# Gated mix of linear attention and a GLU on one core: the down products leave PSUM through ScalarE and are summed in DRAM by accumulating transfers, where VectorE summed them in SBUF

## Chip, cores and metric

The kernel runs on one core of a Trainium2 chip. The metric is the device time of one execution in microseconds (us). Lower is better.

## What is computed

Two branches read the same input x (2048 tokens of 640 numbers, float32) and a gate per token mixes them:

```python
g = sigmoid((x * gate_w).sum(-1, keepdims=True))
a = linear_attention(x, wqkv, wo)        # 32 heads of 20, phi(t) = where(t > 0, t + 1, exp(t)) + 1e-6
b = (sigmoid(x @ w_gate) * (x @ w_up)) @ w_down     # 640 -> 1536 -> 640
return g * a + (1 - g) * b
```

The change concerns b, above all its last product ("down"), and the way b comes to the final mix.

## The kernel before

**Layout.** Everything is kept transposed: features on the 128 partitions, tokens along the free axis. 640 features are KC = 5 chunks of 128, 1536 hidden features are FC = 12 blocks of 128, and 2048 tokens are NG = 4 groups of TG = 512. Groups are worked in pairs, the pair pr = 1 (groups 2 and 3) first and then pr = 0 (groups 0 and 1). A float32 operand is split into a high part (ScalarE copy to fp32r) and a low part (VectorE subtraction), and each product is three matmuls: high by high, high by low, low by high (`mm3`, L183 to L187).

**Stages.** First the keys. Then for each pair a q phase (`q_phase`, L1252), which makes phi(q) and stores it in DRAM (`p_dram`; in the q phase of pr = 1 the small matrix M, the heads' key-value products times wo, is made as well and written to `m_dram`), and an f phase (`f_phase`, L1271). The f phase walks through the 12 hidden blocks f. For each it takes seven steps s1 to s7 that make the gate and up products of both groups, with partial sums of the operands formed beforehand by VectorE. Steps s1, s3 and s5 each leave something in the PSUM tile "ch" that ScalarE copies out before TensorE goes on in the same tile: the copy of s1 has to be done before s3 starts, with s2 between them.

**The down product.** After s5 of each f from 2 on, five down units are worked (L1309 to L1312): one token group, all five output chunks o. A unit is `down_unit` (L1240): six matmuls with the weights of two hidden blocks, into a PSUM tile "rot" or "dd" (two buffers each). Its result is added to b of that group and chunk: the first pair of hidden blocks (f = 0) is copied by ScalarE into the SBUF tile `tb`, every later one is added to `tb` by VectorE (L1246 to L1250). So there are 20 batches of five units, ten in each f phase. The last two hidden blocks are done by `last_down` (L1331): ten units in a row, the first halves of the first four of them ahead. That makes 120 units in all. In the pair pr = 1, `last_down` also sends each finished chunk of `tb` to `b_dram` (L1342, issued by GpSimd), since `tb` is used again by the pair pr = 0.

**Between the pairs.** `last_down` of pr = 1 runs just ahead of the q phase of pr = 0. Around it ScalarE makes the high parts that this phase needs: `wgh` (the q weights), `xbh`, `b12h` (parts of x); VectorE then the low parts, and from x in the staging tile `xst` the operand sums. When the last of them has been split (`xth`, `xtl`), SP loads the other half of x into the same staging tile (L314).

**The final mix.** For the groups 2, 3, 0, 1 in this order: 25 products M times phi(q) for each group; `scale_b` (L1485) multiplies b by 1 - g (`omg`, read back from `om_dram`); `finish` (L1488) adds the PSUM tile to it, and SP stores it. Groups 2 and 3 read b from `b_dram` (`load_b`, L1447), groups 0 and 1 have it in `tb`. The loads for the third and fourth group are issued after the products of the second and third (L1534 to L1538).

**What sets the order.** The program is written in the order in which each engine runs it. A planner (`Order`, L46) keeps estimated clocks of TensorE, ScalarE and VectorE and drops waiting operand preparations (splits, sums) between the fixed steps where its estimates say that they fit. Each helper (`act`, `vec2` and so on) adds its cost to these clocks, so an operation that changes engine can move others. Each engine runs its list strictly in order. Transfers are issued by SP, except those from tiles that GpSimd issues (`p_dram`, `m_dram`, `om_dram`, `b_dram`). Tiles with `bufs=n` rotate: a writer waits until the last user of the buffer is done.

Of the kernel before, what the change touches and what calls it, by code (L numbers as in the profile page):

```python
# [7 lines left out]
F32 = mybir.dt.float32  # L8
F32R = mybir.dt.float32r
I32 = mybir.dt.int32  # L10
AF = mybir.ActivationFunctionType
OP = mybir.AluOpType
# [3 lines left out]
P = 128  # L16
S, D, F = 2048, 640, 1536
H, DH = 32, 20
KC = D // P
FC = F // P  # L20
TG = 512
NG = S // TG
# [134 lines left out]
def v_cost(w):  # L157
    return 0.155 + w * 0.00104
# [3 lines left out]
def gated_mix_kernel(ctx: ExitStack, tc: tile.TileContext, xt, xn, wk, wv, wo, wst_q, wst_f, out_t):  # L162
    nc = tc.nc
# [4 lines left out]
    dram = ctx.enter_context(tc.tile_pool(name="scratch", bufs=1, space=DRAM))  # L168
# [5 lines left out]
    def width(ap):  # L174
        n = 1
        for s in ap.shape[1:]:
            n *= s
        return n

    def ps_tile(tag):  # L180
        return psum.tile([P, 512], F32, name=tag, tag=tag, bufs=2)
# [7 lines left out]
    def prod(out, terms, first):  # L189
        for n, t in enumerate(terms):  # L190
            mm3(out, *t, first and n == 0, n == len(terms) - 1)


    def act(out, src, fn, after="", **kw):
        order.on_act(width(out), after)
        nc.scalar.activation(out, src, fn, **kw)  # L196

    def vec2(out, a, b, op, after=""):
        order.on_vec(width(out), after)
        nc.vector.tensor_tensor(out, a, b, op=op)  # L200
# [21 lines left out]
    def add(out, a, b, after=""):  # L222
        vec2(out, a, b, OP.add, after)
# [12 lines left out]
    logit_l = common.tile([P, S // P], F32R, name="logit_l")  # L236
    fac = common.tile([P, NG, TG], F32, name="fac")
    p_dram = dram.tile([P, KC, NG, TG], F32, name="p_dram")
    b_dram = dram.tile([P, KC, 2, TG], F32, name="b_dram")
    om_dram = dram.tile([P, NG, TG], F32, name="om_dram")  # L240
    m_dram = [dram.tile([D, D], F32, name=n) for n in ("mh_dram", "ml_dram")]
    bdn = HPG * DH
# [468 lines left out]
    g = GTBatch(0, [0])  # L711
# [8 lines left out]
    for c in range(1, 4):  # L720
# [66 lines left out]
        g = GTBatch(c, batches[c])  # L787
# [44 lines left out]
    def tt(name, dt=F32, shape=(P, TG)):  # L832
        return pw.tile(list(shape), dt, name=name, tag="t", bufs=4)

    def ct(name, dt=F32, shape=(P, TG)):
        return pw.tile(list(shape), dt, name=name, tag="c", bufs=5)
# [320 lines left out]
    down_pool = []  # L1157
    HT, DST, WD = {}, {}, {}
    d_loads = [n for n in entries if n[0] == "f"]
    tb = None  # L1160

    def load_d():
        if d_loads:
            n = d_loads.pop(0)
            t = down_pool[0].tile([P, D], F32, name="dst", tag="dst", bufs=2)
            nc.sync.dma_start(t, wst_f[n[2], :, 2])
            DST[n] = (t, order.pe + 4.0)
# [10 lines left out]
    def queue_d(n):  # L1178
        if not down_pool:
            waiting_d.append(n)  # L1180
            return
        order.add(a_cost(D), v_cost(D), lambda: split_d(n), ("d", n), lambda: DST[n][1])
# [9 lines left out]
    other = []  # L1192

    def m_close():
        nonlocal tb
        mp_cm.__exit__(None, None, None)
        m1_cm.__exit__(None, None, None)
        kp_cm.__exit__(None, None, None)
        down_pool.append(ctx.enter_context(tc.tile_pool(name="down", bufs=1, reuse_waits="tile")))
        tb = down_pool[0].tile([P, KC, 2, TG], F32, name="tb")  # L1200
        load_d()
        load_d()
        for n in waiting_d:
            queue_d(n)
        xst2 = down_pool[0].tile([P, 2, KC, CW], F32, name="xst2", tag="xst2")
        other.extend(Next(0, i, xf, i * CW, xst2, True) for i in range(2))
        other[0].load()
# [27 lines left out]
    def down_term(ps, pr, f, o, g, first):  # L1235
        os_ = slice(o * P, (o + 1) * P)
        h, l = WD["f", pr, f]
        mm3(ps, h[:, os_], l[:, os_], *HT[f, g], first, not first)

    def down_unit(pr, f, o, g, ps=None):  # L1240

        if ps is None:
            ps = ps_tile("rot" if (o + g) % 2 else "dd")
            down_term(ps, pr, f, o, g, True)
        down_term(ps, pr, f + 1, o, g, False)
        dst = tb[:, o, g]  # L1246
        if f == 0:
            act(dst, ps, AF.Copy, "p")
        else:
            add(dst, ps, dst, "p")  # L1250

    def q_phase(pr, b12, extra):  # L1252

# [77 lines left out]
    def last_down(pr, units):  # L1331
        order.need(("d", ("f", pr, FC - 1)))
        early = []
        for i in units[:4]:
            g, o = divmod(i, KC)
            early.append(ps_tile("rot" if (o + g) % 2 else "dd"))
            down_term(early[-1], pr, FC - 2, o, g, True)
        for i in units:
            g, o = divmod(i, KC)
            down_unit(pr, FC - 2, o, g, early.pop(0) if early else None)  # L1340
            if pr:
                nc.gpsimd.dma_start(b_dram[:, o, g], tb[:, o, g])  # L1342
            order.fill()

    order.need((nx[1], 2))
# [60 lines left out]
    groups = (2, 3, 0, 1)  # L1406
    PL, PQ, BL, OMG, MHL = {}, {}, {}, {}, {}

    def x2_tile(name, dt=F32):
        return px.tile([P, 2, TG], dt, name=name, tag="x2", bufs=10)  # L1410

    def x3_tile(name, dt=F32):
        return px.tile([P, 3, TG], dt, name=name, tag="x3", bufs=4)
# [18 lines left out]
    def load_p(g):  # L1432

        if groups.index(g) % 2 == 0:
            t = down_pool[0].tile([P, KC, TG], F32, name="pl", tag="xst2")
            nc.sync.dma_start(t, p_dram[:, :, g])
            PL[g] = [t[:, u] for u in range(KC)]
        else:
            PL[g] = []
            for u in range(0, KC, 2):  # L1440
                t = x2_tile("pl")
                w = min(2, KC - u)
                nc.sync.dma_start(t[:, :w], p_dram[:, u:u + w, g])
                PL[g] += [t[:, i] for i in range(w)]
        PL[g, "at"] = order.pe + 6.0

    def load_b(g):  # L1447

        OMG[g] = tt("omg")
        nc.sync.dma_start(OMG[g], om_dram[:, g])  # L1450
        if g < 2:
            BL[g] = [tb[:, o, g] for o in range(KC)]
        elif g == groups[0]:
            BL[g] = [ct("bl") for _ in range(KC)]
            for o in reversed(range(KC)):
                nc.sync.dma_start(BL[g][o], b_dram[:, o, g - 2])
        else:
            t = [x3_tile("bl") for _ in range(2)]
            nc.sync.dma_start(t[0], b_dram[:, 0:3, g - 2])
            nc.sync.dma_start(t[1][:, 0:2], b_dram[:, 3:5, g - 2])  # L1460
            BL[g] = [t[o // 3][:, o % 3] for o in range(KC)]

    def pq_scale(g, u):
        p = PL[g][u]
# [2 lines left out]
    def pq_tiles(g):  # L1467

        if groups.index(g) % 2 == 0:
            t = [x2_tile("pq", F32R) for _ in range(5)]  # L1470
            PQ[g] = [(t[u // 2][:, u % 2], t[2 + u // 2][:, u % 2]) for u in range(4)] + [(t[4][:, 0], t[4][:, 1])]
        else:
            t2 = [x2_tile("pq", F32R) for _ in range(2)]
            t3 = [x3_tile("pq", F32R) for _ in range(2)]
            PQ[g] = [tuple(t[:, u] for t in t2) for u in range(2)] + [tuple(t[:, u] for t in t3) for u in range(3)]

    def queue_scale(g, lazy=False):
        for u in range(KC):
            order.add(0, v_cost(TG), lambda u=u: pq_scale(g, u), ("sc", g), lambda: PL[g, "at"], lazy=lazy)

    def queue_pq(g):
        for u in range(KC):
            order.add(a_cost(TG), v_cost(TG), lambda u=u: split(*PQ[g][u], PL[g][u]), ("pq", g, u))

    def scale_b(g, o):  # L1485
        vec2(BL[g][o], BL[g][o], OMG[g], OP.mult)
# [24 lines left out]
    last_down(0, range(2 * KC))  # L1511
    load_p(groups[2])
    load_b(groups[1])
    for gi, g in enumerate(groups):
        for u in range(KC):
            order.need(("pq", g, u))
        for o in reversed(range(KC)):
            order.add(0, v_cost(TG), lambda o=o: scale_b(g, o), ("b", g, o), first=True)
        if 0 < gi < NG - 1:
            nxt = groups[gi + 1]  # L1520
            queue_scale(nxt)
            pq_tiles(nxt)
            queue_pq(nxt)
        for o in range(KC):
            os_ = slice(o * P, (o + 1) * P)
            cuts = (0, TG // 2, TG) if gi == NG - 1 and o == KC - 1 else (0, TG)
            for c0, c1 in zip(cuts, cuts[1:]):
                ps = ps_tile(("rot", "dd", "cc", "ch")[(o + gi) % 4])
                prod(ps[:, c0:c1], [(MHL[k, 0][:, os_], MHL[k, 1][:, os_], PQ[g][k][0][:, c0:c1],
                                     PQ[g][k][1][:, c0:c1]) for k in range(KC)], True)  # L1530
                order.need(("b", g, o))
                finish(g, o, ps, c0, c1)
            order.fill()
        if gi == 1:  # L1534
            load_p(groups[3])
            load_b(groups[2])
        if gi == 2:
            load_b(groups[3])  # L1538
    for cm in (pw_cm, pg_cm, px_cm):
        cm.__exit__(None, None, None)  # L1540

# [39 lines left out]
```

## Time and profile before

| What | us |
|---|---|
| median of 3 runs (764.15 to 766.01) | 765.08 |
| the profiled execution, its own time | 766.16 |
| span of the profiled execution (first to last instruction) | 764.4 |
| VectorE busy | 559.7 |
| ScalarE busy | 327.1 |
| GpSimd busy | 26.9 |

The profile is that of one execution. The span is 1.8 us shorter than that execution's own time, and that execution is 1.1 us above the median of the runs. "Busy" counts an engine's instructions; a matmul's row ends when its pipeline has drained, so consecutive matmul rows overlap, and the distance from start to start is what one costs. In the rows of a timeline the columns are the start, the duration, the engine, the line of the program, the operation with output <- inputs, the count, and in brackets how long the engine had been idle before it and what ended that.

### The profile page before, as it was taken

Reading aid. Unit: us, or ns where it says so; the run is one execution under the profiler, and the core shown is the slowest. Engines: PE = TensorE matmul, PEld = TensorE weight load, DVE = VectorE, ACT = ScalarE, POOL = GpSimd, SP = SyncE. Lnnn points to the kernel's source line nnn. Section 1 sums busy time; section 2 is a strip of 40 time slices with the busy share of each in tenths; the row PEclk is TensorE's granted clock in tenths of the full one; section 3 lists DMA queues with packets and bytes.
Section 4 is the critical chain, followed back from the end, with each engine's and each line's share of the span. In section 5 each row is a group of like instructions: output and inputs, shape, how many; then the busy total and the mean of one; then the engine's idle time right before and its main releaser. Section 6 shows DMA issues by size and latency. Waiting matters only on the chain.

```text
span 764.4 us, 9852 instructions
## 1 busy us (share of the span) xinstructions
PE 757.3 (99%) x3727; PEld 649.2 (85%) x3727; DVE 559.7 (73%) x988; ACT 327.1 (43%) x603; POOL 26.9 (4%) x55
## 2 busy tenths in 40 slices
PE   9999999999999999999999999999999999999998
PEld 7999999988888888888888878888888888888886
DVE  4888778877776677678878766666776788777664
ACT  4763646356554524333434445555333334231110
POOL 0000000023000000000001210000000000000000
PEclk9999999999999999999999999999999999999999
DMA  7130414597722212121322354322121222455233
GB/s 259 50 123 2 138 37 137 167 273 249 238 97 76 97 49 69 35 84 34 117 69 104 135 186 141 108 76 96 36 69 34 84 104 73 120 178 193 83 128 121
DMA packets 44725, 85.40 MB, mean 112 GB/s; under 512 B 8055, under 2 KB 20855, under 8 KB 44677
## 3 DMA queue, kind: packets, MB, share of 16 engines
q1 hardware_dynamic: 41061, 72.57, 29.4%
q0 software_dynamic: 3616, 12.19, 4.5%
q8 instruction: 29, 0.48, 0.2%
q14 instruction: 19, 0.16, 0.1%
HBM read 67.32 MB, written 17.43 MB: 111 GB/s over the span
## 4 chain that ended last, share of the span: by engine, by line
PE 98%; DMA 1%; ACT 0%; DVE 0%; SPq 0%; issue 0%
PE dd L186 9%; PE dd L185 9%; PE dd L184 9%; PE ch L184 9%; PE ch L185 9%; PE ch L186 9%; PE rot L184 8%; PE rot L185 8%; PE rot L186 8%; PE cc L184 6%; PE cc L186 6%; PE cc L185 6%; DMA wv_sb<-wv 1%; PE ch L1124 1%; DMA xnh<-wk 0%; PE rot L1024 0%
## 5 line engine op out<-in xcount | busy, mean ns | idle before, releaser
L196 ACT ACTIVATE c<-ch 128x512 f32<-128x512 f32 x72 | 43.0, 598 | 151.6 <-PE ch L186 151.4
L200 DVE TENSOR_TENSOR hl<-c,hh 128x512 fp32r<-128x512 f32 x48 | 33.0, 688 | 27.7 <-ACT hh L196 27.7
L196 ACT ACTIVATE c<-c 128x512 f32<-128x512 f32 x48 | 30.1, 628 | 44.6 <-DVE c L200 44.6
L186 PE MATMUL rot<-hh,wdl 128*128 128x512 f32 x120 | 46.8, 390 | 0.0
L186 PE MATMUL dd<-hh,wdl 128*128 128x512 f32 x120 | 46.8, 390 | 0.0
L184 PE MATMUL dd<-hh,wdh 128*128 128x512 f32 x120 | 46.7, 389 | 0.0
L184 PE MATMUL rot<-hh,wdh 128*128 128x512 f32 x120 | 46.7, 389 | 0.0
L185 PE MATMUL dd<-hl,wdh 128*128 128x512 f32 x120 | 46.7, 389 | 0.0
L185 PE MATMUL rot<-hl,wdh 128*128 128x512 f32 x120 | 46.7, 389 | 0.0
L200 DVE TENSOR_TENSOR c<-cc,c 128x512 f32<-128x512 f32 x48 | 32.9, 685 | 18.8 <-ACT c L196 13.8
L200 DVE TENSOR_TENSOR tb<-rot,tb 128x512 f32<-128x512 f32 x52 | 35.8, 688 | 8.9 <-PE rot L186 8.3
L184 PE MATMUL dd<-xrh,wgh 128*128 128x512 f32 x102 | 40.0, 393 | 1.8 <-ACT wgh L196 1.8
L200 DVE TENSOR_TENSOR wsl<-wsum,wsh 128x512 fp32r<-128x512 f32 (+1 forms) x48 | 36.0, 753 | 7.2 <-ACT wsh L196 7.1
L200 DVE TENSOR_TENSOR tb<-dd,tb 128x512 f32<-128x512 f32 x52 | 35.7, 686 | 6.8 <-PE dd L186 6.3
L186 PE MATMUL dd<-xrh,wgl 128*128 128x512 f32 x102 | 39.9, 391 | 0.1
L185 PE MATMUL dd<-xrl,wgh 128*128 128x512 f32 x102 | 39.8, 390 | 0.0
L196 ACT ACTIVATE wsh<-wsum 128x512 fp32r<-128x512 f32 (+1 forms) x48 | 31.8, 678 | 17.4 <-DVE wsum L200 17.4
L200 DVE TENSOR_TENSOR wgl<-wst,wgh 128x640 fp32r<-128x640 f32 x32 | 26.3, 822 | 15.3 <-ACT wgh L196 15.3
L186 PE MATMUL ch<-xth,wsl 128*128 128x512 f32 x96 | 37.5, 390 | 0.0
L184 PE MATMUL ch<-xth,wsh 128*128 128x512 f32 x96 | 37.3, 389 | 0.0
L185 PE MATMUL ch<-xtl,wsh 128*128 128x512 f32 x96 | 37.3, 389 | 0.0
L196 ACT ACTIVATE xth<-xst 128x512 fp32r<-128x512 f32 x24 | 14.3, 626 | 47.5 <-DVE xst L200 47.5
(393 smaller groups left out, 2211.4 us busy)
## 6 DMA issues: line engine op xcount, KB each, us to landing
wst<-wst_f SPq DMA_DIRECT2D x24, 640.0 KB, 3.9
xst<-xt SPq DMA_DIRECT2D x12, 640.0 KB, 6.0
dst<-wst_f SPq DMA_DIRECT2D x24, 320.0 KB, 2.9
xnst<-xn SPq DMA_DIRECT2D x16, 320.0 KB, 3.0
p_dram<-qr POOLq DMA_DIRECT2D x20, 256.0 KB, 3.9
pden<-p_dram SPq DMA_DIRECT2D x20, 256.0 KB, 4.1
b_dram<-tb POOLq DMA_DIRECT2D x10, 256.0 KB, 2.6
pl<-p_dram SPq DMA_DIRECT2D x2, 1280.0 KB, 7.4
```

What stands on the lines that cost most here:

```text
L184: nc.tensor.matmul(out, l_hi, r_hi, start=first, stop=False, skip_group_check=True)
L185: nc.tensor.matmul(out, l_hi, r_lo, start=False, stop=False, skip_group_check=True)
L186: nc.tensor.matmul(out, l_lo, r_hi, start=False, stop=last, skip_group_check=True)
L196: nc.scalar.activation(out, src, fn, **kw)
L200: nc.vector.tensor_tensor(out, a, b, op=op)
L1124: nc.tensor.matmul(ps[:w, :w], v[:, m, :w], gt[:, m, c0:c0 + w], start=(m == 0), stop=(m == KC - 1))
```

## The change

Every down unit is now copied out of PSUM by ScalarE into a small tile `y` (four buffers), and GpSimd issues a transfer of `y` to `b_dram`: for the first pair of hidden blocks it overwrites, for all later ones it adds to what is in DRAM. VectorE's additions and the tile `tb` are gone, `b_dram` has room for all four groups, and the final mix reads b of all groups from `b_dram`. The loads of b and phi(q) for the third and fourth group are issued before the products of the second and third group instead of after them.

```diff
-    b_dram = dram.tile([P, KC, 2, TG], F32, name="b_dram")
+    b_dram = dram.tile([P, KC, NG, TG], F32, name="b_dram")
...
-        tb = down_pool[0].tile([P, KC, 2, TG], F32, name="tb")
...
         down_term(ps, pr, f + 1, o, g, False)
-        dst = tb[:, o, g]
-        if f == 0:
-            act(dst, ps, AF.Copy, "p")
-        else:
-            add(dst, ps, dst, "p")
+        y = y_tile("y")
+        act(y, ps, AF.Copy, "p")
+        nc.gpsimd.dma_start(b_dram[:, o, 2 * pr + g], y, accum_op=OP.add if f else OP.bypass)
+
+    def y_tile(name):
+        return down_pool[0].tile([P, TG], F32, name=name, tag="y", bufs=4)
...
             down_unit(pr, FC - 2, o, g, early.pop(0) if early else None)
-            if pr:
-                nc.gpsimd.dma_start(b_dram[:, o, g], tb[:, o, g])
...
-        if g < 2:
-            BL[g] = [tb[:, o, g] for o in range(KC)]
-        elif g == groups[0]:
-            BL[g] = [ct("bl") for _ in range(KC)]
+        n = groups.index(g)
+        if n == 1:
+            t = [x3_tile("bl") for _ in range(2)]
+            nc.sync.dma_start(t[0], b_dram[:, 0:3, g])
+            nc.sync.dma_start(t[1][:, 0:2], b_dram[:, 3:5, g])
+            BL[g] = [t[o // 3][:, o % 3] for o in range(KC)]
+        else:
+            def tile_of(tag):
+                return down_pool[0].tile([P, TG], F32, name="bl", tag=tag, bufs=4)
+
+            if n == 0:
+                BL[g] = [ct("bl") for _ in range(KC)]
+            elif n == 2:
+                BL[g] = [tile_of("hh") for _ in range(4)] + [tile_of("hl")]
+            else:
+                BL[g] = [tile_of("hl") for _ in range(3)] + [y_tile("bl") for _ in range(2)]
             for o in reversed(range(KC)):
-                nc.sync.dma_start(BL[g][o], b_dram[:, o, g - 2])
...
+                nc.sync.dma_start(BL[g][o], b_dram[:, o, g])
...
+        if gi == 1:
+            load_p(groups[3])
+            load_b(groups[2])
+        if gi == 2:
+            load_b(groups[3])
         for o in reversed(range(KC)):
             order.add(0, v_cost(TG), lambda o=o: scale_b(g, o), ("b", g, o), first=True)
...
-        if gi == 1:
-            load_p(groups[3])
-            load_b(groups[2])
-        if gi == 2:
-            load_b(groups[3])
```

More of the change, by code (lines that the diff above doesn't have):

```diff
@@ L1159, in gated_mix_kernel @@
     d_loads = [n for n in entries if n[0] == "f"]
-    tb = None
     def load_d():
@@ L1194, in m_close @@
     def m_close():
-        nonlocal tb
         mp_cm.__exit__(None, None, None)
@@ L1450, in load_b @@
         nc.sync.dma_start(OMG[g], om_dram[:, g])
-        if g < 2:
-            BL[g] = [tb[:, o, g] for o in range(KC)]
-        elif g == groups[0]:
-            BL[g] = [ct("bl") for _ in range(KC)]
-            for o in reversed(range(KC)):
-                nc.sync.dma_start(BL[g][o], b_dram[:, o, g - 2])
[L1457 to L1461, printed above, removed]
+        n = groups.index(g)
[13 more added lines that the diff above has]
+                BL[g] = [tile_of("hl") for _ in range(3)] + [y_tile("bl") for _ in range(2)]
+            for o in reversed(range(KC)):
+                nc.sync.dma_start(BL[g][o], b_dram[:, o, g])
     def pq_scale(g, u):
```

## The prediction

> **What bounds the kernel now.** I read the page's busy times first, then the chain that ended last, then TensorE's waits.
>
> ```profile
> span 764.4 us, 9852 instructions
> ...
> PE 757.3 (99%) x3727; PEld 649.2 (85%) x3727; DVE 559.7 (73%) x988; ACT 327.1 (43%) x603; POOL 26.9 (4%) x55
> ```
> ```profile
> PE 98%; DMA 1%; ACT 0%; DVE 0%; SPq 0%; issue 0%
> ```
> ```profile
> PE dd L184 <- ACT wgh L196: 1.8, 1, 1.8
> ```
> TensorE is busy 757.3 of 764.4 us and is 98% of the chain. Of its 7.1 idle us the longest single wait in mid-run is one of 1.8 us, for ScalarE's `wgh`. As built, the changed kernel gives TensorE the same matmuls in the same order. So VectorE's saving cannot shorten anything by itself: the change can win at most this 1.8 us, and can lose wherever TensorE meets a later ScalarE or a later transfer. (0.2% of 765.08, 1.53 us, is about what a measurement of this kernel can tell from no change.)
>
> **What is removed and added on the engines.**
>
> ```profile
> L200 DVE TENSOR_TENSOR tb<-rot,tb 128x512 f32<-128x512 f32 x52 | 35.8, 688 | 8.9 <-PE rot L186 8.3
> L196 ACT ACTIVATE tb<-rot 128x512 f32<-128x512 f32 x10 | 6.0, 599 | 3.4 <-PE rot L186 3.0
> ```
> Half of the units come from a rot tile and half from a dd tile; these are the rot rows, and the dd ones are like them. Of the 60 + 60 units, 10 + 10 are copied by ScalarE already and 50 + 50 are VectorE additions (the other 2 in the row belong to the final mix). VectorE loses 100 x 0.688 = 68.8 us, ScalarE gains 100 x 0.599 = 59.9 us and goes from 43% to 51%. Neither is the bound. What counts is whether ScalarE is late, and the trace already has two batches of units (f = 2 and 3 of each pair, which end the pair of hidden blocks f = 0) with ScalarE copies in just the order of the new program:
>
> ```profile
> 246.88 0.60 ACT L196 ACTIVATE tb<-rot 128x512 f32<-128x512 f32 x1 [0.24 <-PE rot L186]
> ...
> 252.33 0.60 ACT L196 ACTIVATE tb<-rot 128x512 f32<-128x512 f32 x1
> 252.82 0.73 ACT L196 ACTIVATE wdh<-dst 128x640 fp32r<-128x640 f32 x1
> 253.69 0.60 ACT L196 ACTIVATE c<-ch 128x512 f32<-128x512 f32 x1
> ```
> ```profile
> 255.54 0.39 PE L184 MATMUL ch<-xth,wuh 128*128 128x512 f32 x1
> ```
> The fifth copy starts 5.45 us after the first (252.33 - 246.88). The copy of "ch" that TensorE needs ends at 254.29, 1.25 us ahead of s3 at 255.54. So the ScalarE work by itself costs nothing in the 20 batches; TensorE's own work hides it.
>
> **The new wait.** `y` has four buffers, so the fifth copy of a batch waits until the first transfer has landed, and on ScalarE the split of `wdh` and the copy of "ch" are queued behind it. ScalarE can slip by the 0.14 us that it idles ahead of "ch" (253.69 less 252.82 + 0.73) and the 1.25 above: 1.4 us. From the end of a copy to its buffer's release there are thus 5.45 - 0.60 = 4.85 us before ScalarE waits, and 4.85 + 1.4 = 6.2 us before TensorE does. Now the transfer:
>
> ```profile
> 417.68 0.69 DVE L200 TENSOR_TENSOR tb<-dd,tb 128x512 f32<-128x512 f32 x1 [0.67 <-PE dd L186]
> ```
> ```profile
> 418.67 0.54 POOL L1342 DMA_DIRECT2D b_dram<-tb  x1 [0.82 <-DVE tb L200]
> ```
> ```profile
> 598.54 0.54 POOL L1054 DMA_DIRECT2D om_dram<-om  x1 [134.47 <-ACT om L196]
> ```
> ```profile
> DMA  0000000000000009997988981000000703000000
> ...
> q0 software_dynamic: 80, 0.26, 23.1%
> ...
> om_dram<-om POOLq DMA_DIRECT2D x1, 256.0 KB, 2.5
> ```
> The first two rows: GpSimd starts 0.30 us after the operation that it waits for (418.67 - 418.37). The other two fences are a plain write of the same 256 KB that is alone, and the 3.0 us from 598.5 on: the transfer engines are busy from slice 15 on (0.075 us each, so 1.08 us after the issue), the write holds all 16 of them for T = 23.1% of 3.0 = 0.7 us, and it lands after 2.5, some 0.7 after its data. A release thus takes 0.30 + 1.08 + T + 0.7 = 2.1 + T: 2.8 us for a plain write.
>
> **What an accumulating transfer holds the engines for is not in this trace.** From below, T = 0.7: the write alone, if the read of b went beside it. From above:
>
> ```profile
> pden<-p_dram SPq DMA_DIRECT2D x20, 256.0 KB, 4.1
> ```
> a read of 256 KB lands after 4.1 us; a read and a write one behind the other, with nothing overlapped, make T = 4.1 + 2.5 = 6.6. It has to fetch 256 KB from DRAM besides moving the 256 KB of `y`, by the same 16 engines; two passes at the row's 0.7 are 1.4. I take T = 1.5, near the row of the plain write, since many packets are in flight at a time. The Trainium skill ("Collectives: The Full Stack", section "The bandwidth ceiling: the fold count and why AG ≠ RS ≠ AR") holds that an add in the transfer path is free, but needs two source reads on one ring, which halves the rate; that would be T = 1.4 as an estimate, and by it the sum below would be 1.3 us in place of 1.9, where the write's row alone gives none; no run here shows it yet. With T = 1.5 the release takes 3.6 us, inside the 4.85: the 20 batches cost nothing.
>
> **The place where it does cost: `last_down` ahead of the q phase of pr = 0.** There ten units come in a row, the second halves of the first four in quick succession, and six transfers queue up before the tenth copy can start.
>
> ```profile
> 413.85 0.39 PE L186 MATMUL dd<-hh,wdl 128*128 128x512 f32 x1
> ```
> ```profile
> 424.05 0.40 PE L186 MATMUL rot<-hh,wdl 128*128 128x512 f32 x1
> ```
> These are the last matmuls of units 1 and 10; a copy starts 0.03 us after such a row ends, as the fifth copy of the batch above does at 252.33:
>
> ```profile
> 251.90 0.40 PE L186 MATMUL rot<-hh,wdl 128*128 128x512 f32 x1
> ```
> The first copy runs from 414.27 to 414.87, and its data starts at 414.87 + 0.30 + 1.08 = 416.25. With transfers behind each other at T each, the sixth lands at 416.25 + 6T + 0.7, and the tenth copy, due at 424.48, needs that buffer: it is late by D = 6T - 7.53 us, if that is positive. For T = 1.5 that is 1.47. A load shares the engines at that time:
>
> ```profile
> q1 hardware_dynamic: 144, 0.33, 7.2%
> ```
> (stretch 414 to 427): the q weights hold the engines for 0.94 us. It may fall wholly behind the sixth transfer or wholly ahead of it; I take half, 0.47. So D = 1.9 us. What is queued behind the tenth copy on ScalarE is the second `b12h`, and from it a chain without slack:
>
> ```profile
> 425.69 0.69 DVE L200 TENSOR_TENSOR b12l<-xs,b12h 128x512 fp32r<-128x512 f32 x1
> 426.29 2.14 DVE L200 TENSOR_TENSOR xst<-xst 128x512 f32<-128x512 f32 x3
> ...
> 435.24 0.69 DVE L200 TENSOR_TENSOR xtl<-xst,xth 128x512 fp32r<-128x512 f32 x1 [0.70 <-ACT xth L196]
> ```
> ```profile
> 435.96 1.24 SPq L314 DMA_DIRECT2D xst<-xt  x2
> ```
> ```profile
> 453.80 0.50 PE L184 MATMUL dd<-xrh,wgh 128*128 128x512 f32 x1 [1.77 <-ACT wgh L196]
> ```
> The sums of x follow `b12l`, the last `xtl` frees the staging tile, SP loads it, the sums from it and their splits precede `wgh` on ScalarE, and there TensorE waits its 1.8 us. With D = 0 the new order reaches the second `b12l` at about 425.6 and the last `xtl` at about 435.2, as before (one more `xth` stands ahead of the table load, one less behind). So this wait becomes 1.8 + D. The other `last_down` has nothing of this kind behind its tenth copy: the copies delay `pq` splits of the second group, whose products come a whole group later.
>
> **Moved loads.** b of two more groups (10 x 256 KB) comes from DRAM, issued ahead of the products of the second and third group.
>
> ```profile
> 726.58 0.69 DVE L200 TENSOR_TENSOR bl<-dd,bl 128x512 f32<-128x512 f32 x1 [2.75 <-PE dd L186]
> 734.53 3.10 DVE L200 TENSOR_TENSOR tb<-tb,omg 128x512 f32<-128x512 f32 x5 [7.26 <-DMA omg<-om_dram]
> ...
> 761.15 0.42 DVE L200 TENSOR_TENSOR tb<-ch,tb 128x256 f32<-128x256 f32 x1 [1.36 <-PE ch L186]
> ```
> ```profile
> bl<-b_dram SPq DMA_DIRECT2D x1, 768.0 KB, 9.5
> ```
> VectorE waited 7.26 us for `omg` here and TensorE did not notice; the loads now start one group of products earlier, and loads like them landed after 9.5 (last fence), ahead of their use. Stores queue behind them on SP, and nobody waits for a store. The last addition waits for TensorE, and no load stands behind it. Zero, then; if this cover were gone, the cost is bounded by the 7 us. GpSimd issues 110 transfers more, 110 x 0.54 = 59 us of an idle engine; the `p_dram` and `om_dram` writes stand behind some of them on GpSimd and would be late only if the queue does not keep up (rival 3).
>
> **Sum.** 764.4 + 1.9 = 766.3 us of span, 766.16 + 1.9 = 768.1 for that execution, which lay 1.1 above the median; on the median 765.08 + 1.9 = **767.0 us**.
>
> **Rivals.**
> 1. *Nothing happens*: T below 1.25, so D = 0: 765.1 us. For it: a plain write takes 0.7. Against it: twice the data to read.
> 2. *Faster*: VectorE, without its ten additions between 414 and 425, forms the operand sums earlier, SP's load at 435.96 moves up, and the 1.8 us wait goes: 763.3 us. It decides from a load 1.8 us earlier on. Against it: the sums stand behind `b12h`, which now stands behind the tenth copy.
> 3. *The queue does not keep up*: a block lasts 245.25 - 226.19 = 19.06 us (rows below) and brings five transfers, so from T = 3.8 on the transfers set the pace of the 20 blocks. At T = 5: 20 x (25 - 19.06) = 119, and D = 22: about 906 us. For it: the upper bound of 6.6.
>
> ```profile
> 226.19 0.23 PE ch L186
> ...
> 245.25 0.23 PE ch L186
> ```
> **How the numbers follow.** Forecast (T from 1.25 to 3.8) 0.56, rival 1 0.24, rival 2 0.08, rival 3 0.12. Of the forecast, 0.10 lies below T = 1.43, within 0.2% even with half of the load's share. Faster 0.08, same 0.24 + 0.10 = 0.34, slower 0.46 + 0.12 = 0.58. Range: from 764.4, half a clearing of the wait, to T = 3.8 (D = 15.7): 781. It leaves out rival 3 and most of rival 2, at most 0.20. The forecast's own range is 765.1 to 781.
>
> **What would show it.** TensorE free of waits in the batches; the fifth copy of a batch at its old place; transfers of `y` landing after about 3.3 us alone; copies nine and ten before the q phase late and the wait for `wgh` at 1.8 + D. It is wrong if landings stay near 2.5 (rival 1), if the x load moves up (rival 2), or if ScalarE waits for transfers in every batch (rival 3).

## The result, and the profile after

| | before | after |
|---|---|---|
| median, us (4 runs each) | 764.82 | 773.32 |
| lowest to highest, us | 764.15 to 766.01 | 772.66 to 776.44 |
| profiled execution: own time, span | 766.16, 764.4 | 773.57, 771.8 |

The changed kernel is slower: ratio 1.0117, 95% interval 1.0087 to 1.0148, about 8.5 us. Direction and range of the forecast held (767.0, range 764.4 to 781), but it expected 1.9 us.

The page of the changed kernel: span, busy time, one DMA queue (packets, MB, share of the 16 engines' span), one group of instructions, and one kind of transfer (count, size, median us to landing).

```profile
span 771.8 us, 10181 instructions
...
PE 759.5 (98%) x3727; PEld 649.1 (84%) x3727; DVE 499.8 (65%) x888; ACT 385.5 (50%) x703; POOL 118.8 (15%) x165
...
q0 software_dynamic: 18816, 41.04, 27.2%
...
L1245 POOL DMA_DIRECT2D b_dram<-y x120 | 97.4, 833 | 370.3 <-ACT y L196 368.8
...
b_dram<-y POOLq DMA_DIRECT2D x120, 256.0 KB, 6.8
```

VectorE lost 59.9 us and ScalarE gained 58.4 (68.8 and 59.9 were worked out from single rows, which overlap where they follow each other closely); by themselves neither shows in the time (experiment 1). What is new is the transfer: GpSimd's queue holds the engines for 27.2% of the span, and a transfer of `y` lands 6.8 us after its issue. TensorE's waits in the changed kernel (total us, times, longest):

```profile
PE dd L184 <- ACT wgh L196: 3.4, 2, 2.2
PE rot L271 <- POOL warm L268: 1.4, 1, 1.4
PE dd L184 <- ACT y L196: 1.3, 1, 1.3
PE rot L184 <- ACT y L196: 1.2, 2, 0.9
PE rot L185 <- DVE b12l L200: 0.3, 1, 0.3
PE rot L184 <- ACT b12h L196: 0.3, 1, 0.3
PE cc L1100 <- DVE ms L200: 0.3, 1, 0.3
```

The second line is the start, the same as before; the last one lies at 191 us, ahead of all transfers of `y`. The others come from two places, the two `last_down` stages. **Where the 7.4 us of span went** can be read off because TensorE runs the same matmuls in the same order in both kernels: take the same matmul in both timelines and subtract. The difference is its lag. First before, then after:

```profile
410.68 0.39 PE L184 MATMUL dd<-hh,wdh 128*128 128x512 f32 x1
...
438.06 0.40 PE L184 MATMUL dd<-xrh,wgh 128*128 128x512 f32 x1
...
440.13 0.39 PE L184 MATMUL dd<-xah,wgh 128*128 128x512 f32 x1
...
691.92 0.39 PE L184 MATMUL rot<-pq,m 128*128 128x512 f32 x1
...
760.83 0.28 PE L186 MATMUL ch<-pq,m 128*128 128x256 f32 x1
```

```profile
409.31 0.39 PE L184 MATMUL dd<-hh,wdh 128*128 128x512 f32 x1
...
429.18 0.38 PE L184 MATMUL rot<-b12h,wgh 128*128 128x256 f32 x1 [0.30 <-ACT b12h L196]
...
440.25 0.62 PE L184 MATMUL dd<-xrh,wgh 128*128 128x512 f32 x1 [2.24 <-ACT wgh L196]
440.67 0.63 PE L185 MATMUL dd<-xrl,wgh 128*128 128x512 f32 x1
...
444.10 0.40 PE L184 MATMUL dd<-xah,wgh 128*128 128x512 f32 x1
...
457.16 0.50 PE L184 MATMUL dd<-xrh,wgh 128*128 128x512 f32 x1 [1.12 <-ACT wgh L196]
...
694.02 0.50 PE L184 MATMUL dd<-hh,wdh 128*128 128x512 f32 x1 [1.32 <-ACT y L196]
...
698.52 0.50 PE L184 MATMUL rot<-pq,m 128*128 128x512 f32 x1 [0.91 <-ACT y L196]
...
767.57 0.28 PE L186 MATMUL ch<-pq,m 128*128 128x256 f32 x1
```

| same matmul, before / after | lag of after | added |
|---|---|---|
| 410.68 / 409.31 | -1.37 | (start) |
| 438.06 / 440.25 | +2.19 | 3.56: waits for `b12h`, `b12l`, `wgh` |
| 440.13 / 444.10 | +3.97 | 1.78: the same matmuls, run slower |
| 453.80 / 457.16 | +3.36 | -0.61: this wait is 1.12 instead of 1.77 |
| 691.92 / 698.52 | +6.60 | 3.24: `last_down` of pr = 0 |
| 760.83 / 767.57 | +6.74 | 0.14: the whole final mix |
| span 764.4 / 771.8 | +7.4 | 0.66: the last stores |

The 1.37 us at the start arise among the first matmuls, which the change does not touch; the profiled execution of before was 1.3 us above its median. Without them the change costs 3.56 + 1.78 - 0.61 = 4.73 us around the q phase, 3.24 us in the last `last_down`, 0.80 us behind it: 8.8 us, against 8.5 between the medians. Nothing is lost in the 20 batches: from 230 to 410 and from 460 to 690 us the lag is constant.

ScalarE in the two places (timeline of the changed kernel):

```profile
412.96 0.60 ACT L196 ACTIVATE y<-dd 128x512 f32<-128x512 f32 x1 [0.70 <-PE dd L186]
...
417.82 0.60 ACT L196 ACTIVATE y<-dd 128x512 f32<-128x512 f32 x1 [2.22 <-DMA b_dram<-y]
...
424.32 0.60 ACT L196 ACTIVATE y<-dd 128x512 f32<-128x512 f32 x1 [0.17 <-DMA b_dram<-y]
...
428.01 0.60 ACT L196 ACTIVATE y<-rot 128x512 f32<-128x512 f32 x1 [2.57 <-DMA b_dram<-y]
428.50 0.62 ACT L196 ACTIVATE b12h<-xs 128x512 fp32r<-128x512 f32 x1
...
687.35 0.60 ACT L196 ACTIVATE y<-rot 128x512 f32<-128x512 f32 x1
693.37 0.60 ACT L196 ACTIVATE y<-dd 128x512 f32<-128x512 f32 x1 [5.42 <-DMA b_dram<-y]
```
```profile
439.36 1.24 SPq L314 DMA_DIRECT2D xst<-xt  x2
```

The fifth copy of each stage waits for the first transfer, and so on. In the prediction's rows the tenth copy was due 424.48 - 414.27 = 10.21 us after the first, so here at 423.17; it starts at 428.01, **D = 4.84 us** late. SP's load of x stands at 439.36 instead of 435.96: 3.40 later, 4.77 with the 1.37 at the start. So the chain handed D on one for one.

A view by stretches (stretch and its length; busy time and count of TensorE, its weight loads, VectorE, ScalarE, GpSimd; TensorE's granted clock; DMA share; GB/s) of the changed kernel shows the slower matmuls as a granted clock of 0.95 between 425 and 460 us:

```profile
425.00:460.00 35.00, 30.86 (x147) 24.99 (x146) 19.63 (x30) 18.01 (x33) 5.56 (x9) 0.95 0.52 147
```

### The profile page after: what moved, and what is told of

Read it like the earlier page. It is cut to its first block, busy times and chain, and to the rows that moved or that the text cites. A ratio compares the mean times of both kernels' runs of the same rounds, so it can differ in the third digit from the quotient of the medians.

```text
span 771.8 us, 10181 instructions
## 1 busy us (share of the span) xinstructions
PE 759.5 (98%) x3727; PEld 649.1 (84%) x3727; DVE 499.8 (65%) x888; ACT 385.5 (50%) x703; POOL 118.8 (15%) x165
## 3 DMA queue, kind: packets, MB, share of 16 engines
q0 software_dynamic: 18816, 41.04, 27.2%
## 4 chain that ended last, share of the span: by engine, by line
issue 42%; PE 35%; POOL 12%; DMA 5%; DVE 4%; ACT 2%; POOLq 0%; SPq 0%; ACTq 0%; DVEq 0%
POOL b_dram L1245 11%; PE rot L184 3%; PE rot L185 3%; PE rot L186 3%; PE ch L185 3%; PE ch L184 3%; PE ch L186 3%; PE dd L186 3%; PE dd L185 3%; PE dd L184 2%; PE cc L184 2%; PE cc L186 2%; PE cc L185 2%; DMA b_dram<-y 2%; DMA xst<-xt 2%
## 5 line engine op out<-in xcount | busy, mean ns | idle before, releaser
L1245 POOL DMA_DIRECT2D b_dram<-y x120 | 97.4, 833 | 370.3 <-ACT y L196 368.8
L196 ACT ACTIVATE y<-dd 128x512 f32<-128x512 f32 x60 | 35.9, 599 | 31.5 <-PE dd L186 20.3
L196 ACT ACTIVATE y<-rot 128x512 f32<-128x512 f32 x60 | 36.0, 599 | 25.9 <-PE rot L186 18.1
L973 POOL DMA_DIRECT2D p_dram<-qr x20 | 11.2, 559 | 212.6 <-DVE qr L204 203.1
```

Source lines behind the costliest of these rows:

```text
L973: nc.gpsimd.dma_start(p_dram[:, u, g], r)
L1245: nc.gpsimd.dma_start(b_dram[:, o, 2 * pr + g], y, accum_op=OP.add if f else OP.bypass)
```

## The experiments

Theory A: the transfers hold the four buffers of `y` too long, and only in the two `last_down` stages does that reach TensorE. Rival B: the transfers hold the 16 engines so long that other loads are late, however many buffers there are. Rival C: the copies make ScalarE late by themselves.

**1. Eight buffers.**

```diff
-        return down_pool[0].tile([P, TG], F32, name=name, tag="y", bufs=4)
+        return down_pool[0].tile([P, TG], F32, name=name, tag="y", bufs=8)
```

> Eight buffers for y instead of four, all else as in the changed kernel. Theory A (the loss is ScalarE waiting for a buffer of y in the two last_down stages: a transfer holds its buffer too long for four of them; 4.8 us ahead of the q phase of pr = 0, 3.2 us in the last_down of pr = 0): the copies 5 to 10 wait for transfers that landed long ago, no wait of ScalarE for a transfer of y is left, TensorE's waits for y and b12h go, the matmuls of 0.63 us at the q phase go, and the time comes back to that of before, 764 to 766 us. Rival B (the transfers hold the 16 DMA engines so long that the loads of x and of the final mix come late, however many buffers there are): at least half of the loss stays, 769 us or more. Rival C (the copies themselves make ScalarE late): no change, 773 us.

Measured: 766.0 us (12 runs), ratio to before 1.002 (1.0005 to 1.0034). The waits of TensorE:

```profile
PE ch L1124 <- DMA wv_sb<-wv: 1.7, 1, 1.7
PE dd L184 <- ACT wgh L196: 1.4, 1, 1.4
...
```

No wait for `y`, `b12h` or a second `wgh` is left. B and C are out as the main cause of the loss: the same copies and the same transfers cost 1.1 us (2.6 at the upper end of the interval) once the buffers suffice. These 1.1 us over before stay open; the wait for `wv_sb` lies at 162 us, ahead of all transfers of `y`, and of the other kernels' profiles some have it (1.4 to 1.5 us) and some do not.

**2. No adding.** `accum_op=OP.bypass` for all transfers; the kernel then leaves out the sum of the parts of b.

> All transfers of y write b plainly instead of adding to it (this leaves out the sum of the parts of b). Theory A: a plain write holds the engines for about 0.7 us instead of about 1.75, so four buffers are enough: 764 to 766 us, no TensorE wait for y. Rival B: the same, 764 to 766, since the transfers then hold the engines for 120 x 0.7 us only. Rival C (copies on ScalarE as such): no change, 773 us.

Measured: 765.16 us, ratio 1.0007 (0.9996 to 1.0018), as A has it; one wait of 0.3 us for `y` is left. Its page, with the same queue line of before behind it, gives the price of the adding (before had 10 transfers of b where there are 120 now, and 100 of these add):

```profile
span 763.5 us, 10181 instructions
...
q0 software_dynamic: 12416, 41.04, 14.1%
...
b_dram<-y POOLq DMA_DIRECT2D x120, 256.0 KB, 2.7
```
```profile
q0 software_dynamic: 3616, 12.19, 4.5%
```

Plain: (14.1% of 763.5 - 4.5% of 764.4) / 110 = 0.67 us of all engines per transfer. Adding: (27.2% of 771.8 - 14.1% of 763.5) / 100 = 1.02 us on top, so T, the time for which one adding transfer holds the engines, is 1.69 us; and 6400 packets more, 64 each.

**3 and 4. One place at a time.** `OP.bypass` for the ten transfers of one `last_down` only, whose part of the sum is then left out. This is the edit of 3; 4 has `pr == 0` in it:

```diff
-        nc.gpsimd.dma_start(b_dram[:, o, 2 * pr + g], y, accum_op=OP.add if f else OP.bypass)
+        nc.gpsimd.dma_start(b_dram[:, o, 2 * pr + g], y, accum_op=OP.bypass if f == 0 or (pr == 1 and f == FC - 2) else OP.add)
```

> Only the ten transfers of the last_down ahead of the q phase of pr = 0 write plainly (this leaves out the sum there); all others add. Theory A, with the lag of TensorE read by place: minus 4.8 us, 768.5 us; the waits for b12h and the first wgh and the slow matmuls behind it go, the waits in the other last_down (2.5 us) stay. Rival B (engines held in general): less than 2 us of gain, 771.5 or more.

> Only the ten transfers of the last_down of pr = 0, ahead of the final mix, write plainly (this leaves out the sum there); all others add. Theory A: minus 3.2 us, 770.1 us; TensorE's waits for y (2.5 us in three) go, those around the q phase stay as in the changed kernel. Together with the run where the other last_down writes plainly the gains should add up to about 8 us. Rival B: the loads of the final mix share the engines with the transfers and keep the copies late even so, less than 1 us of gain, 772.5 or more.

Measured: 768.97 us (ratio 1.0065, 1.0048 to 1.0081) and 770.92 (1.0091, 1.0072 to 1.0111): gains of 4.35 and 2.4 us, expected 4.8 and 3.2. Together 6.75, where 8 was expected, of the 8.5. In the second kernel TensorE still loses 0.98 us in the last `last_down`, with plain transfers, and the fifth copy there is still 4.28 us late:

```profile
691.23 0.60 ACT L196 ACTIVATE y<-dd 128x512 f32<-128x512 f32 x1 [4.28 <-DMA b_dram<-y]
```

So most of that one copy's wait is not the adding's; but the copies behind it then wait 0.47 us in all, against 4.25 in the changed kernel.

**5 and 6. Three and five buffers.** `bufs=3`, `bufs=5`.

> Three buffers for y instead of four. Theory A (the price is the wait for a buffer): the first transfer of a batch landed 3.95 us after its issue (413.85 to 417.8), and the issue comes 0.3 us after the copy ends, so a buffer comes free about 4.3 us after its copy. In a batch the fourth copy is due 3.5 us after the first has ended and is some 0.8 us late, the fifth 1 to 2 us; ScalarE has 1.25 us of slack ahead of TensorE there, so each of the 18 adding batches costs 0 to 1 us, and each last_down some 1.7 us more with a slower clock behind it: 777 to 795 us. Rivals B (engines held) and C (copies): no change, 773 us.

> Five buffers for y instead of four. Theory A, from the changed kernel's rows: the tenth copy ahead of the q phase then waits for the fifth transfer (landed by 424.3) and not for the sixth (428.0), due at 423.1, so it is late by 1.2 us and not by 4.9, and the clock does not drop there; in the other last_down the first wait falls on the sixth copy, 1.36 us later, and TensorE waits 1 us and not 2.5. 773.3 - 3.5 - 1.5 = 768.3 us, ratio 1.0045 to 1.005. Rivals B (engines held) and C (copies): no change, 773 us.

Measured: 786.87 us (ratio 1.0288, 1.0265 to 1.0311) and 769.48 (1.0063, 1.0040 to 1.0085). So 3, 4, 5, 8 buffers give 787, 773, 769.5 and 766 us. With five, the tenth copy was 2.5 us late (426.54 against 413.83 + 10.21), not 1.2, and TensorE's second wait for `wgh` grew to 2.3 us and dropped the clock; both had been expected smaller, and the median is 1.2 us above what was expected (the profiled execution, at 772.36, is the slowest of the six).

**7. The load that shares the engines ahead of the q phase**, moved behind the load of x.

```diff
-            if u % 2 or u == KC - 1:
+            if (u % 2 or u == KC - 1) and (pr, u) != (0, 1):
                 order.then(load_w)
...
-    q_phase(0, lambda k: [(c_h[c][:, k], c_l[c][:, k]) for c in range(2)], {})
+    q_phase(0, lambda k: [(c_h[c][:, k], c_l[c][:, k]) for c in range(2)], {4: [load_w]})
```

> The changed kernel, four buffers, with the one load that shares the engines with the transfers ahead of the q phase (320 KB of q weights, not used until 453) issued behind the load of x at 439 instead of at 421.9. Theory (it held the engines for 0.93 us in the 3.8 us between the landings of the fifth and the sixth transfer): the sixth lands 1 to 2 us earlier, the tenth copy is late by 3 to 3.9 us and not by 4.9, and the time falls by 1 to 2 us, to 771.3 to 772.3, a little more where the clock then does not drop. Rival (the transfers are that slow by themselves): under 0.5 us, 773 us.

Measured: 772.45 us, ratio 1.0104 (1.0081 to 1.0128), against the 1.0117 of the changed kernel. First and tenth copy in its timeline:

```profile
415.12 0.60 ACT L196 ACTIVATE y<-dd 128x512 f32<-128x512 f32 x1 [0.70 <-PE dd L186]
...
428.55 0.60 ACT L196 ACTIVATE y<-rot 128x512 f32<-128x512 f32 x1 [0.80 <-DMA b_dram<-y]
```

Late by 428.55 - 425.33 = 3.2 us instead of 4.84: the load is worth 1.6 us of D. In time only 0.9 us shows, and the two intervals overlap; in its profiled execution the lag at the second `wgh` had gained 1.9 us, and an earlier wait at 191 us, which the edit does not touch, had lost more than that. The gain in time is not settled, the one in D is.

**8. The loads that share the engines in the last `last_down`**, issued behind the load of p of the third group.

```diff
     load_m(4)
-    load_b(groups[0])
...
     load_p(groups[2])
+    load_b(groups[0])
     load_b(groups[1])
```

> The changed kernel, four buffers, with the loads of b and omega for the first group of the final mix issued behind the load of p of the third group instead of ahead of the last_down of pr = 0 (1.5 MB that then shares no engines with the first transfers of y there). Theory (the fifth copy there waits 5.42 us and not 2.22 as in the other last_down because these loads share the 16 engines): its wait falls to 2 to 3 us, TensorE's waits for y in that place fall from 2.5 us to under 0.7, 2 us less, 771 us. Rival (the transfers are as slow by themselves): waits unchanged, 773 us. Third: the loads come too late for the first group and the final mix waits for them, 774 us or more.

Measured: 777.01 us, ratio 1.0164 (1.0138 to 1.0189): the third outcome. The fifth copy's wait did fall, from 5.42 to 2.53 us:

```profile
694.30 0.60 ACT L196 ACTIVATE y<-dd 128x512 f32<-128x512 f32 x1 [2.53 <-DMA b_dram<-y]
```

but the sixth copy, at 698.04, then waited 2.62 us instead of 0.81. TensorE's waits for `y` went from 2.5 to 1.7 us only, not to the expected 0.7, and at 722 it waited 2.08 us for a part of `pq`, and the clock dropped. So these loads lengthen the wait there, and this is no place to put them.

**9. Loads of the final mix back at their old place**, behind the products of the second and third group.

> The changed kernel with the loads of p and b of the third and fourth groups of the final mix put back behind the products of the second and third group, where they were before. Prediction on record (moved loads cost nothing) and theory A: no change, 773 us, ratio 1.010 to 1.0125, lag of TensorE constant from 700 us on. Rival (the moved loads crowd the transfers and cost part of the loss): 771 us or less. Third (put back they come too late): over 775.

Measured: 780.24 us, ratio 1.0197 (1.0171 to 1.0222). I expected no change; the third outcome came. SP's queue in its timeline, then VectorE:

```profile
716.47 17.57 SPq L1494 DMA_DIRECT2D out_t<-bl  x6
734.13 1.44 SPq L1439 DMA_DIRECT2D pl<-p_dram  x3
...
736.13 3.79 SPq L1464 DMA_DIRECT2D bl<-b_dram  x5
```
```profile
745.97 3.10 DVE L200 TENSOR_TENSOR bl<-bl,omg 128x512 f32<-128x512 f32 x5 [12.30 <-DMA bl<-b_dram]
```

At the old place the loads stand behind stores on SP, and each store waits for its product; VectorE then waits 12.3 us for b and TensorE 2.39 us for `pq` at 754. Before, groups 0 and 1 had b in SBUF. The move costs nothing, as the prediction had it; but without it the change loses nearly twice as much.

**10. The clock, in the kernel before.** ScalarE makes one copy three times, which lengthens the one wait that is there:

```diff
-            def wg_split(n, src):
+            def wg_split(n, src, more=0):
...
+                for _ in range(more):
+                    nc.scalar.activation(W[n, 0][0], src, AF.Copy)
                 split(*W[n, 0], src)
...
-            wg_split(("q", pr, u), WST[n][:, u % 2])
+            wg_split(("q", pr, u), WST[n][:, u % 2], 2 if (pr, u) == (0, 4) else 0)
```

> The kernel BEFORE, with ScalarE making the copy of wgh for the last q unit pair of pr = 0 three times instead of once (two idle repetitions, about 0.63 us each, ahead of the wait at 453.8). It lengthens the one stall of TensorE from 1.8 to about 3.0 us and changes nothing else. Theory (a stall of 2 us or more drops TensorE's clock: eight or nine matmuls of 0.63 us behind it, 1.75 us more): 1.25 + 1.75 = 3.0 us over before, ratio 1.0039, and rows of 0.63 us behind the stall. Rival (the slow matmuls in the changed kernel come from the transfers or from what is computed there): 1.25 us only, ratio 1.0016, rows of 0.39 us.

Measured: 766.4 us, ratio 1.0017 (1.0005 to 1.0030): the rival's number; but the rows are the theory's.

```profile
452.79 0.79 PE L184 MATMUL dd<-xrh,wgh 128*128 128x512 f32 x1 [3.21 <-ACT wgh L196]
453.38 0.63 PE L185 MATMUL dd<-xrl,wgh 128*128 128x512 f32 x1
...
458.51 0.62 PE L185 MATMUL dd<-xal,wgh 128*128 128x512 f32 x1
```

The mean granted clock of every run tells the two apart. Of 74 runs of before beside the experiments, 37 have 0.999 or 1.000 and a median of 763.7 us, 37 have 0.997 or 0.998 and 765.5. The mean doesn't say where the clock dropped, but run 12 below, without that wait, has no run under 0.999: so before's own wait of 1.8 us very likely drops the clock in about half of its executions. With the longer wait 11 of 12 runs are below 0.999, with a median of 766.5, which is 2.8 above the undropped 763.7; the expected 3.0 had been set against all runs of before. The twelfth has 1.000 and 763.4 us, so even this wait seems not to drop the clock each time. The drop has its price, then, and about half of it was in the reference already.

**11 and 12. A version that beats both?** The sum `tb` took 20 KB per partition, `y` with eight buffers takes 16; the difference and what was free make room for a second staging tile of x (10 KB), so that the x behind the 1.8 us wait can be loaded early. The line with `setattr` is in 12 only.

```diff
-        xst2 = down_pool[0].tile([P, 2, KC, CW], F32, name="xst2", tag="xst2")
-        other.extend(Next(0, i, xf, i * CW, xst2, True) for i in range(2))
+        xst2 = [down_pool[0].tile([P, 2, KC, CW], F32, name="xst2", tag="xst2", bufs=2) for _ in range(2)]
+        other.extend(Next(0, i, xf, i * CW, xst2[i], True) for i in range(2))
...
     tail = f_phase(1, {
+        (2, 2): [lambda: other[1].load()],
...
     nx[0].queue_sums()
-    order.add(0, 0, lambda: nx[1].load(lag=7.0))
+    order.add(0, 0, lambda: setattr(nx[1], "at", order.pe + 7.0))
     nx[1].queue_sums()
```

> Eight buffers for y, and in the room that the sum of b left in SBUF a second staging tile for x, so that the x of the second column half is loaded in the third block of pr = 1 instead of behind the last split of the first half. Theory: TensorE's last mid-run wait, 1.8 us for wgh at 453, is set by that load, so it goes: 1.4 to 1.8 us less than the kernel with eight buffers alone (766.0), 764.3 us, and about 763.3 or ratio 0.998 against before if that kernel's own 1.1 us over before is chance. Rival (something else is then late on the same chain, ScalarE's or VectorE's own work): the wait for wgh stays over 1 us and the time stays at 766.

> Eight buffers for y and the second staging tile for x as in the run with both, but with the sums of the second column half given to the planner 7 us later than in that run, so that VectorE and ScalarE make them behind the split of wgh for the fourth q unit pair and not ahead of it. Theory: in the run with both, the wait of 1.0 us for wgh at 448 came from those sums, which started 5 us earlier than before; now neither wait for wgh is left, TensorE has no wait above 0.5 us between 200 and 760 us, the clock does not drop, and the time is 763.0 to 764.0 us, ratio 0.997 to 0.9995. Rival: another operation on that chain is late instead and a wait of about 1 us stays, 764.4 us, ratio 0.9995 to 1.001.

Measured: 764.37 us, ratio 1.0006 (0.9986 to 1.0025), for the first: the wait at 453 went, but the sums, now early, stood ahead of another `wgh`, and TensorE waited 1.0 us at 448. With the sums at their old time: **763.36 us, ratio 0.9981 (0.9969 to 0.9994)**. All its waits:

```profile
PE rot L271 <- POOL warm L268: 1.4, 1, 1.4
PE cc L1100 <- DVE ms L200: 0.5, 1, 0.5
```

All 12 runs have a clock of 0.999 or 1.000. The gain over before is 1.3 us, 0.2%. In its profile TensorE gains 2.5 us in the place of the wait (lag -1.61 to -4.08 against before's profile); the kernel with eight buffers alone was 1.1 us slower than before, and why stays open. The change itself gives only the room, and whether before could find that room otherwise wasn't tried.

## Why the prediction was right, and where its sizes were off

- **TensorE bounds, its order stays, nothing to win but 1.8 us**: the first two held; its rows are matched one for one above. The third is somewhat low: the rows were those of an execution in which the clock stayed up behind the wait, and in half of the others it seems to drop there, which is worth another 1.8 us (experiments 10 to 12).
- **The 20 batches cost nothing**: held. ScalarE waited for a transfer in one batch only (1.7 us at 582), and TensorE not at all. The margin was smaller than thought: the first transfer of an adding batch lands 3.8 to 4.3 us after its issue, not 3.3, so its buffer comes free after 4.1 to 4.6 of the 4.85 us; in the batch at 577 it landed after 4.7, and there ScalarE waited. The first transfer of the stage ahead of the q phase, issued at 413.85, is like the others; that of the last `last_down`, beside the loads of the final mix, landed after 7.1.

```profile
b_dram<-y POOLq DMA_DIRECT2D x1, 256.0 KB, 3.9
```

- **Slower through the tenth copy ahead of the q phase, with a loss of D**: held in place and mechanism, wrong in size: D was 4.84 us, not 1.9. Two terms of D = 6T - 7.53 + load were mis-sized. The load of q weights was taken at half of its 0.94 us; taking it away shortens D by 1.6. The rest, 3.2 = 6T - 7.53, gives T = 1.8 in place of 1.5, near the 1.69 from the queue's shares. With T = 1.69 and a landing 3.9 us after the issue, the fixed part of a landing is about 0.4 us longer than the 1.08 + 0.7 taken; as an estimate that makes D = 6 x 1.69 + 0.4 - 7.53 = 3.0 without the load. The bound from below, 0.7, was much nearer to the truth than 6.6, but the value taken was still low. By the rule of the Trainium skill named in the prediction ("Collectives: The Full Stack", section "The bandwidth ceiling: the fold count and why AG ≠ RS ≠ AR") it would have been, as an estimate, 1.4, twice a plain write; the runs show 1.69 / 0.67 = 2.5 times.
- **"This wait becomes 1.8 + D"**: the sum held (4.73 of loss for D = 4.84), the place did not. TensorE met the late operands earlier, at `b12h` (429.18) and at the first `wgh` (440.25), then ran 3.85 us at the lower clock, and the wait named came out shorter, 1.12 us. As the load of x sets that point anyway, neither the earlier waits nor the lower clock added to the loss there.
- **"The other `last_down` has nothing of this kind behind its tenth copy"**: this step failed, and 3.24 us with it. It looked at what is queued behind the tenth copy and not at the copies themselves: they empty the PSUM tiles "rot" and "dd", two buffers each, which TensorE needs for the following units. In the first `last_down` the fifth copy is late by 2.22 us and TensorE has that slack; in the last one by 5.42, and TensorE waits at 694.02. It is 5.42 there mostly because the transfers share the engines with loads of the final mix: 2.53 without those of b and omega, but still 4.28 with plain writes. The adding makes the copies behind it late too, and with them TensorE: it loses 0.98 us there with plain writes and 3.4 with adding ones (3.24 and the 0.14 behind).
- **Moved loads: zero**: right for the place where the change puts them (lag +6.60 to +6.74 over the whole final mix). The old place costs 7 us more.
- **GpSimd's issue 0.54 us each**: an adding one took 0.86; nobody waited for that.
- **Rivals**: 1 (nothing) needed T below 1.25. 2 (faster) needed the load of x earlier; it came 3.4 us later. 3 (the queue does not keep up) needed T of 3.8; TensorE lost nothing in the batches. (Half a clearing of the wait, which the range's lower end stands for, is 764.2 rather than 764.4; nothing hangs on it.)

## What to carry to other kernels

An accumulating transfer takes work from an engine, but what it charged here is the time for which it holds its source buffer: count the buffers from the stretch where its producers come fastest, with whatever else loads there, not from the average rate. Ask of each delayed copy out of PSUM not only what is queued behind it but which matmul needs its bank. And when an addition in SBUF goes, it is the freed room that may be worth something: here it bought the removal of another wait.

## What the runs showed of the hardware that was not expected

- A transfer of 256 KB that adds to DRAM held the 16 engines for 1.69 us, a plain one for 0.67; GpSimd took 0.86 and 0.54 us to issue them.
- Short waits lower TensorE's clock. Between 400 and 760 us of all profiles, each of the 12 single waits of 1.96 us or more was followed within 2 us by matmuls at 0.43 us from start to start instead of 0.23, mostly for 3.4 to 3.9 us (6 us behind the waits of 3.21 and 2.39); of four between 1.69 and 1.81 us two were. In run 8 two waits close together, 1.15 and 0.34 us at 431.5 and 432.2, were followed by it as well. A drop costs 1.5 to 1.9 us, and the two long ones 2.9. The Trainium skill ("TensorE: Matmul & The Clock Gate", section "What's actually happening") has the gate close after an idle window of some 3.4 us that runs freely; the length of most drops and the chance in them (37 of 74 runs of before) would fit such a window, but waits of 2 us, well short of it, were enough here.
